# Joining the small matrix products of both tiles of a chunk into common runs, in a DeltaNet and GELU kernel

## The chip, the cores and the metric

The kernel runs on one core of a Trainium2 chip. The metric is the time of one execution on the device, in microseconds (us). The engines are named as the profile names them: PE (TensorE, matrix products; PEld is its loading of weights), DVE (VectorE), ACT (ScalarE), POOL (GpSimd) and SP (SyncE, which issues most transfers). Each engine works through its own list of instructions in order and waits on semaphores for the others. Matrix products land in PSUM, which DVE and ACT empty.

## The reference

There are two stages. The first is a delta-rule attention over 4 batches, 8 heads, 768 steps and a head width of 48; the second is a feed-forward block over the resulting 3072 x 384 matrix, with an exact GELU between its two products.

```
for t in range(S):
    y[:, :, t] = einsum('bhd,bhde->bhe', q[:, :, t], state)
    v_old = einsum('bhde,bhd->bhe', state, kt)      # kt: the normed key
    state = state + bt * einsum('bhd,bhe->bhde', kt, vt - v_old)
x = y.transpose(0, 2, 1, 3).reshape(B * S, H * D)
h = x @ w_in                                        # 384 x 2048
out = (0.5 * h * (1 + erf(h / sqrt(2)))) @ w_out    # 2048 x 384
```

All is fp32 (the two weights arrive as 8-byte floats and are decoded to fp32 on the chip). Each fp32 matrix product of the program stands in the trace as two MATMUL records.

## The kernel before

The steps are cut into 12 chunks of 64. A tile is one chunk of two batches: 8 heads, 48 wide, with the 64 steps of one batch on the lower and of the other on the upper half of the 128 partitions. A chunk has two tiles (`NA = 2`), called a0 and a1 below. Two chunks make a group. Inside a chunk the recurrence is written as small products, one for each head and half:

- `transposed` (L276) turns K and Q of a tile (psT, 128 x 128 transposes); `products` (L286) makes K K^T and K Q^T at once (psG, the Gram products). ACT copies the K K^T half to `G` (L301), `pack` (L309) copies three pieces of `G` into `diag`, DVE masks the other half into `P` (L307).
- `eliminate_steps` (L339) inverts the 32 x 32 diagonal blocks of a whole group on DVE: one transpose and one multiply over 1024 columns, 30 pairs of multiply and add (L359, L361), three transposes back (L370, L374). `join` (L391) then makes the 64 x 64 inverses from the 32 x 32 ones by two levels of 32 x 32 products (psJ, L404 and L407). Each call does one chunk of the group: DVE scales the first level (L415), ACT copies the second (L419).
- `against_state` (L450) is K S (psK) and then two DVE operations that give W (L459, L460); `query` (L477) is Q S (psQ), copied by ACT to y (L485); `solve` (L463) is U (psU), copied by ACT in four pieces (L475); `next_state` (L503) is K^T U (psS), added to the state by DVE (L512); `read` (L487) is P^T U (psY), added to y by DVE in four pieces (L501); `turn` (L514) transposes the result for the feed-forward block (psX).

The feed-forward block of a chunk is `fc1` (L532: 16 times three products of 128 x 128 with 256 columns, psH, then GELU on ACT, L538) and `fc2` (L540: 32 products with 384 columns, psO). The products of the attention use only part of the PE: 64 x 64 or 32 x 32 of its 128 x 128. In the text a tiled run is a stretch of such products between two stretches of full-size ones (psH, psO, and the transposes psT and psX).

PSUM holds two buffers of two banks for all tiled products (`dn`), two banks for psT and psX (`sq`) and two for psH and psO (`mlp`). The program first writes chunk 0 in an order by hand (L581 to L648), then a plan (L659 to L686) gives each step a due time in chunks, and sorts all steps by it: `state_steps`, `gram_steps` and `join_steps` return (weight, step) pairs that `at` spreads between two times. DVE keeps that order; for the other engines a scheduler orders the instructions as their inputs come free. The weights are decoded on DVE and ACT (`decode`, `signed`, L186 to L208) during chunks 0 and 1.

Of the kernel before, what the change touches and what calls it, by code (L numbers as in the profile page):

```python
# [8 lines left out]
F32 = mybir.dt.float32  # L9
# [7 lines left out]
def kernel(  # L17
# [28 lines left out]
    nc = tc.nc  # L46
# [239 lines left out]
    def products(u, part=(0, 1)):  # L286
# [9 lines left out]
        if 0 in part:  # L296
            if u.t == 0:
                Gs[g] = wk.tile([128, 2 * NA, H, C], F32, tag="G", name="G", bufs=1)
            if u.t == 0 and g > 0:
                Ds[g] = wk.tile([128, NU, HB], F32, tag="diag", name="diag", bufs=1)  # L300
            nc.scalar.copy(heads(Gs[g][:, u.t]), psG[:, :, :, 0:C])  # L301
# [7 lines left out]
    def pack(u, copy=nc.scalar.copy):  # L309
        g = u.c // 2  # L310
        span = slice(u.t * H, (u.t + 1) * H)
        copy(Ds[g][:, span], Gs[g][:, u.t, :, 0:HB])
        for p in range(2):
            lower = slice(p * C + HB, (p + 1) * C)
            copy(Ds[g][lower, span], Gs[g][lower, u.t, :, HB:C])
# [3 lines left out]

    def gram(u):  # L320
        products(u)
        pack(u)
# [68 lines left out]
    def join(g, ts, level, copy=nc.scalar.copy):  # L391

        xm, zf, raw = XMs[g], Zf[g % 2], Gs[g].rearrange("q t h n -> q (t h) n")
        gm = gms[g].rearrange("q t h -> q (t h)")
        psJ = dn("psJ")
        us = range(ts[0] * H, (ts[-1] + 1) * H)
        span = slice(us[0], us[-1] + 1)
        for i, u in enumerate(us):
            for p in range(2):
                top = slice(p * C, p * C + HB)  # L400
                low_ = slice(p * C + HB, (p + 1) * C)
                col = slice(i * HB, (i + 1) * HB)
                if level == 0:
                    nc.tensor.matmul(psJ[low_, 0, col], lhsT=raw[top, u, HB:C],  # L404
                                     rhs=xm[top, u, :], start=True, stop=True)
                else:
                    nc.tensor.matmul(psJ[top, 0, col], lhsT=xm[low_, u, :],  # L407
                                     rhs=zf[low_, u, HB:C], start=True, stop=True)
        for p in range(2):
            top = slice(p * C, p * C + HB)  # L410
            low_ = slice(p * C + HB, (p + 1) * C)
            rows = top if level else low_
            src = psJ[rows, 0, 0:len(us) * HB].rearrange("q (u n) -> q u n", n=HB)
            if level == 0:
                nc.vector.tensor_tensor(  # L415
                    xm[low_, span, :], src,
                    gm[low_, span].unsqueeze(2).to_broadcast([HB, len(us), HB]), op=ALU.mult)
            else:
                copy(zf[top, span, HB:C], src)  # L419
# [22 lines left out]
    def state_product(u, x, psum):  # L442

        for j in range(NP):
            for r, p in QUADS:
                rows = slice(r * C, r * C + D)
                nc.tensor.matmul(psum(p, j, r), lhsT=u.KQt[rows, j, p, x, :],  # L447
                                 rhs=St[rows, u.a, p, j, :], start=True, stop=True)

    def against_state(u):  # L450
        u.W = wk.tile([128, H, D], F32, tag="W", name="W")
        gm = gms[u.c // 2][:, u.t]
        if u.c == 0:
            nc.gpsimd.tensor_tensor(u.W, u.V, ng[:, u.a].unsqueeze(2).to_broadcast([128, H, D]),
                                    op=ALU.mult)
            return
        psK = dn("psK")[:, :, 0:NP * D].rearrange("q r (j d) -> q r j d", d=D)
        state_product(u, 0, lambda p, j, r: psK[HALF[p], r, j, :])
        nc.vector.tensor_tensor(heads(u.W), psK, heads(u.V), op=ALU.subtract)  # L459
        nc.vector.tensor_tensor(u.W, u.W, gm.unsqueeze(2).to_broadcast([128, H, D]),  # L460
                                op=ALU.mult)

    def solve(u, copies=(nc.scalar.copy,)):  # L463
        zf = Zf[(u.c // 2) % 2]
        psU = dn("psU")[:, :, 0:DM].rearrange("q p (h d) -> q p h d", d=D)
        for k in range(NP // 2):
            for r in range(2):
                for p, s in SIDES:
                    h = 4 * k + 2 * s + r
                    nc.tensor.matmul(psU[HALF[p ^ s], p, h, :],  # L470
                                     lhsT=zf[HALF[p], u.t * H + h, :], rhs=u.W[HALF[p], h, :],
                                     start=True, stop=True)
        u.U = wk.tile([128, H, D], F32, tag="U", name="U")
        for i, (p, s) in enumerate(SIDES):
            copies[i % len(copies)](pairs(u.U[HALF[p]], s), pairs(psU[HALF[p ^ s], p], s))  # L475

    def query(u):  # L477
        u.y = None
        if u.c == 0:
            return  # L480
        psQ = dn("psQ")[:, :, 0:NP * D].rearrange("q r (k s d) -> q k s r d", s=2, d=D)
        state_product(u, 1, lambda p, j, r: psQ[HALF[p ^ (j % 2)], j // 2, j % 2, r, :])
        u.y = wk.tile([128, H, D], F32, tag="y", name="y")
        for r in range(2):
            nc.scalar.copy(heads(u.y)[:, r], psQ[:, :, :, r, :].rearrange("q k s d -> q (k s) d"))  # L485

    def read(u, copies=(nc.scalar.copy,)):  # L487
        psY = dn("psY")[:, :, 0:DM].rearrange("q p (h d) -> q p h d", d=D)
        for k in range(NP // 2):
            for r in range(2):  # L490
                for p, s in SIDES:
                    h = 4 * k + 2 * s + r
                    nc.tensor.matmul(psY[HALF[p ^ s], p, h, :], lhsT=u.P[HALF[p], h, :],  # L493
                                     rhs=u.U[HALF[p], h, :], start=True, stop=True)
        u.x = wk.tile([128, H, D], F32, tag="x", name="x")
        for i, (p, s) in enumerate(SIDES):
            dst, src = pairs(u.x[HALF[p]], s), pairs(psY[HALF[p ^ s], p], s)
            if u.y is None:
                copies[i % len(copies)](dst, src)
            else:  # L500
                nc.vector.tensor_tensor(dst, src, pairs(u.y[HALF[p ^ s]], s), op=ALU.add)  # L501

    def next_state(u):  # L503
        if u.c == NC - 1:
            return
        psS = dn("psS")[:, :, 0:NP * D].rearrange("q p (j d) -> q p j d", d=D)
        for j in range(NP):
            for r, p in QUADS:
                nc.tensor.matmul(psS[HALF[r], p, j, :],  # L509
# [207 lines left out]
```

## Time and profile before

| | |
|---|---|
| time, three runs | 756.45 us median (755.42 to 761.29) |
| the profiled execution's own time | 755.02 us |
| its span on the core | 753.3 us |
| chunk 0, by hand | to about 60 us |
| decoding of the weights on DVE | to about 141 us |
| first join of a whole group on PE | at 170.70 us |
| last product on PE ends | at about 749 us |

The profile is of one execution, and the sums of the prediction are made against it. Its views: the page's busy shares, the chain of work that ended last, a table of busy time by stretch of time, groups of instructions (line, engine, operation, output<-input, shape, count, then busy us and mean ns of one, then idle time ahead of them and what ended it), a timeline (start, duration, engine, line, operation, output<-input, shape, count of records) and a list of who waited for whom. A MATMUL's duration in the timeline includes its way through the array, so from one group of matmuls to the next the difference of the starts is what counts.

### The profile page before, as it was taken

The numbers are of one execution on the slowest core, as the hardware profiler recorded it, in microseconds if no ns is written. First come the engines' busy times: TensorE is split into PE (matmuls) and PEld (weight loads), VectorE is DVE, ScalarE is ACT, GpSimd is POOL, SyncE is SP. The second block draws the span as 40 slices with busy tenths as digits, with TensorE's granted clock in tenths as the row PEclk, the third lists the DMA queues.
The fourth block names the chain that finished last, engine by engine and source line by source line (L and its number), as shares of the span: only waits on it lengthen the run. The fifth ranks groups of instructions, "written<-read, shape, count | busy, mean of one in ns | idle before, by whom it ended". The sixth has DMA issues, their size and how long they took to land.

```text
span 753.3 us, 19282 instructions
## 1 busy us (share of the span) xinstructions
PE 704.0 (93%) x8532; PEld 508.5 (68%) x8532; DVE 376.4 (50%) x855; ACT 249.4 (33%) x602; POOL 84.7 (11%) x91
## 2 busy tenths in 40 slices
PE   6549786899999999999999999999999999999997
PEld 5347553576687687687587687687687687586774
DVE  6988999996329722329822329822329821210100
ACT  3335633422553134352134352133352132122120
POOL 5051001203110002110012010012020010000000
PEclk9999999998999999999999999999999999999999
DMA  9807544400311101211101211001001000000000
GB/s 150 199 25 206 131 125 129 103 1 19 60 33 23 32 13 32 44 32 23 34 13 32 44 32 23 12 12 23 12 12 23 12 12 2 11 12 1 22 1 21
DMA packets 84515, 32.90 MB, mean 44 GB/s; under 512 B 77328, under 2 KB 80400, under 8 KB 84432
## 3 DMA queue, kind: packets, MB, share of 16 engines
q1 hardware_dynamic: 78384, 26.36, 16.0%
q10 hardware_dynamic: 5952, 5.12, 3.0%
q8 instruction: 67, 1.10, 0.6%
q0 software_dynamic: 96, 0.20, 0.1%
q14 instruction: 16, 0.13, 0.1%
HBM read 26.94 MB, written 4.72 MB: 42 GB/s over the span
## 4 chain that ended last, share of the span: by engine, by line
PE 77%; DVE 19%; issue 2%; DMA 1%; POOL 1%; ACT 0%; ACTq 0%; POOLq 0%; DVEq 0%
PE psO L544 30%; PE psH L535 30%; DVE tmp L359 3%; DVE Nu L361 3%; PE psT L283 2%; PE psG L293 2%; DVE w_e L204 2%; PE psU L470 2%; PE psJ L404 2%; PE psS L509 2%; PE psQ L447 2%; PE psK L447 2%; PE psJ L407 2%; PE psY L493 1%; DVE w_e L194 1%
## 5 line engine op out<-in xcount | busy, mean ns | idle before, releaser
L544 PE MATMUL psO<-w_out_sb,g 128*128 128x384 f32 x768 | 272.9, 500 | 10.2 <-DVE w_out_sb L205 10.2
L535 PE MATMUL psH<-xT,w_in_sb 128*128 128x256 f32 x1152 | 274.9, 388 | 3.4 <-DVE w_in_sb L205 3.0
L535 PEld LDWEIGHTS psH<-xT,w_in_sb 128*128 128x128 f32 x1152 | 213.1, 191 | 37.4 <-DVE w_in_sb L205 3.5
L544 PEld LDWEIGHTS psO<-w_out_sb,g 128*128 128x128 f32 x768 | 140.4, 192 | 97.2 <-DVE w_out_sb L205 15.6
L538 ACT ACTIVATE g<-psH 128x256 f32<-128x256 f32 x192 | 73.5, 383 | 177.4 <-PE psH L535 177.1
L361 DVE TENSOR_TENSOR Nu<-Nu,tmp 128x30 f32<-128x30 f32 (+9 forms) x180 | 61.9, 344 | 6.2
L359 DVE TENSOR_TENSOR tmp<-Nu 128x30 f32<-128x30 f32 (+9 forms) x180 | 61.8, 343 | 5.6
L253 POOL TENSOR_TENSOR n<-n,half 128x16 f32<-128x16 f32 x10 | 29.5, 2947 | 222.6 <-DVE n L242 222.6
L501 DVE TENSOR_TENSOR x<-psY,y 64x192 f32<-64x192 f32 x88 | 31.0, 353 | 42.3 <-PE psY L493 41.4
L307 DVE TENSOR_TENSOR P<-psG,mask 128x512 f32<-128x512 f32 x20 | 13.7, 690 | 72.8 <-ACT G L301 72.7
L512 DVE TENSOR_TENSOR St<-St,psS 128x384 f32<-128x384 f32 x22 | 12.2, 553 | 75.4 <-PE psS L509 75.0
L459 DVE TENSOR_TENSOR W<-psK,V 128x384 f32<-128x384 f32 x22 | 12.2, 555 | 73.6 <-PE psK L447 56.8
L475 ACT COPY U<-psU 64x192 f32<-64x192 f32 x92 | 28.8, 313 | 46.8 <-PE psU L470 46.0
L548 ACT COPY o_sb<-psO 128x384 f32<-128x384 f32 x24 | 11.5, 479 | 89.3 <-PE psO L544 89.3
L293 PE MATMUL psG<-KQt 48*64 48x128 f32 (+1 forms) x896 | 30.4, 286 | 3.9 <-ACT KQt L284 2.7
L522 ACT COPY xT<-psX 128x384 f32<-128x384 f32 x24 | 11.4, 477 | 68.0 <-PE psX L521 67.9
L293 PEld LDWEIGHTS psG<-KQt 48*64 48x64 f32 x896 | 24.9, 157 | 10.6 <-issue 4.8
L284 ACT COPY KQt<-psT 128x512 f32<-128x512 f32 x48 | 26.5, 589 | 9.1 <-PE psT L283 8.6
L383 POOL MEMSET Zf<- 32x512 f32 x23 | 12.2, 529 | 147.5 <-DVE Zf L374 145.5
L404 PE MATMUL psJ<-XM,G 32*32 32x32 f32 x768 | 15.5, 198 | 13.6 <-DVE XM L370 13.6
L415 DVE TENSOR_TENSOR XM<-psJ,gm 32x512 f32<-32x512 f32 (+1 forms) x26 | 16.9, 649 | 20.4 <-PE psJ L404 20.1
L196 ACT ACTIVATE w_e<-w_e,lim 128x384 uint32<-128x384 uint32 (+2 forms) x31 | 19.4, 625 | 23.0 <-DVE w_e L194 22.8
(100 smaller groups left out, 584.9 us busy)
## 6 DMA issues: line engine op xcount, KB each, us to landing
Qp<-in_q_dram SPq DMA_DIRECT2D x48, 96.0 KB, 3.4
V<-in_v_dram SPq DMA_DIRECT2D x48, 96.0 KB, 2.9
w_out_sb<-in_moe_w_in_dram SPq DMA_DIRECT2D x9, 512.0 KB, 5.3
out_dram<-o_sb ACTq DMA_DIRECT2D x48, 96.0 KB, 2.2
Zf<-in_moe_w_out_dram SPq DMA_DIRECT2D x8, 384.0 KB, 3.5
w_raw<-in_moe_w_out_dram SPq DMA_DIRECT2D x8, 384.0 KB, 3.1
Kp<-in_k_dram SPq DMA_DIRECT2D x28, 96.0 KB, 3.1
w_out_sb<-in_moe_w_in_dram SPq DMA_DIRECT2D x6, 256.0 KB, 4.4
```

Source lines behind the costliest of these rows:

```text
L253: nc.gpsimd.tensor_tensor(flat, flat, half, op=ALU.pow)
L284: nc.scalar.copy(u.KQt[:, :, :, x, :], psT.rearrange("q j (p n) -> q j p n", p=2))
L293: nc.tensor.matmul(psG[HALF[p], r, j, cols], lhsT=u.KQt[rows, j, p, 0, :], rhs=u.KQt[rows, j, p].rearrange("q x n -> q (x n)")[:, cols], s ...
L359: nc.vector.tensor_tensor(tmp, nu[:, j + 1:, j:j + 1].to_broadcast([128, n, j]), nu[:, j:j + 1, 0:j].to_broadcast([128, n, j]), op=ALU.mult)
L361: nc.vector.tensor_tensor(nu[:, j + 1:, 0:j], nu[:, j + 1:, 0:j], tmp, op=ALU.add)
L404: nc.tensor.matmul(psJ[low_, 0, col], lhsT=raw[top, u, HB:C], rhs=xm[top, u, :], start=True, stop=True)
L447: nc.tensor.matmul(psum(p, j, r), lhsT=u.KQt[rows, j, p, x, :], rhs=St[rows, u.a, p, j, :], start=True, stop=True)
L475: copies[i % len(copies)](pairs(u.U[HALF[p]], s), pairs(psU[HALF[p ^ s], p], s))
L501: nc.vector.tensor_tensor(dst, src, pairs(u.y[HALF[p ^ s]], s), op=ALU.add)
L535: nc.tensor.matmul(psH, lhsT=w_in_sb[:, m, f * 128:(f + 1) * 128], rhs=xTs[c][:, m, :], start=(m == 0), stop=(m == NM - 1))
L538: nc.scalar.activation(gs[f], psH, ACT.Gelu)
L544: nc.tensor.matmul(u.psO, lhsT=gs[f][:, u.a * 128:(u.a + 1) * 128], rhs=w_out_sb[:, f, :], start=(f == 0), stop=(f == NF - 1))
```

## The change

The small products of both tiles are made one after the other, without full-size products in between, and what belongs together lands in one PSUM buffer: K S and Q S of a tile in one (`psK`), U of both tiles in one (`psU`), P^T U and K^T U of a tile in one (`psY`, `psS`). The Gram products of both tiles follow each other, and ACT now takes only the needed quarter blocks from them. A `join` level does a whole group at once.

```
 def products(u, part=(0, 1)):
...
-            nc.scalar.copy(heads(Gs[g][:, u.t]), psG[:, :, :, 0:C])
+            nc.scalar.copy(heads(Gs[g][:, span]), psG[:, :, :, HB:C])
+            if g > 0:
...
+                nc.scalar.copy(heads(Ds[g][:, span]), psG[:, :, :, 0:HB])
+                for p in range(2):
+                    lower = slice(p * C + HB, (p + 1) * C)
+                    nc.scalar.copy(Ds[g][lower, span], Gs[g][lower, span])
...
-    def pack(u, copy=nc.scalar.copy):
...
-    def gram(u):
-        products(u)
-        pack(u)
+    def grams(us):
+        for u in us:
+            products(u)
...
     def gram_steps(c):
         us = [tiles[c, a] for a in range(NA)]
-        return [(1.0, fn, u) for fn in (transposed, gram) for u in us]
+        return [(1.0, transposed, u) for u in us] + [(2.0, grams, us)]
...
     def join_steps(g):
-        return [(1.0, join, g, (2 * cc, 2 * cc + 1), level)
-                for level in range(2) for cc in range(2)]
+        return [(1.0, join, g, range(2 * NA), level) for level in range(2)]
...
+    def against_state(us):
+        for u in us:
...
+            u.psK = dn("psK")[:, :, 0:2 * NP * D].rearrange("q r (x j d) -> q x r j d", x=2, d=D)
+            for x in range(2):
+                for j in range(NP):
+                    for r, p in QUADS:
+                        rows = slice(r * C, r * C + D)
+                        to = HALF[p ^ (j % 2)] if x else HALF[p]
+                        nc.tensor.matmul(u.psK[to, x, r, j, :], lhsT=u.KQt[rows, j, p, x, :],
+                                         rhs=St[rows, u.a, p, j, :], start=True, stop=True)
+        for u in us:
...
+            nc.vector.tensor_tensor(heads(u.W), u.psK[:, 0], heads(u.V), op=ALU.subtract)
+            nc.vector.tensor_tensor(u.W, u.W, gm.unsqueeze(2).to_broadcast([128, H, D]),
                                     op=ALU.mult)
...
+                nc.scalar.copy(heads(u.y)[:, r], u.psK[:, 1, r])
...
+    def use(us):
+        for u in us:
+            psY = dn("psY")
+            u.psY = quarters(psY[:, :, 0:NP * D])
+            u.psS = psY[:, :, NP * D:2 * NP * D].rearrange("q p (j d) -> q p j d", d=D)
...
+            if u.c > 0:
+                update(u)
...
+    def outputs(us):
+        use(us)
+        for u in us:
+            next_state(u)
+            read(u)
...
     def state_steps(c):
         us = [tiles[c, a] for a in range(NA)]
-        steps = [(1.0, fn, u) for fn in (against_state, query, solve, next_state, read) for u in us]
+        steps = [(3.0, against_state, us), (2.0, solve, us), (3.0, outputs, us)]
         return steps + [(0.5, turn, u) for u in us]
...
     decode(0)
-    solve(first[0], on[0])
     decode(1)
-    solve(first[1], on[1])
+    solve(first[:NA], on)
     signed(0)
-    read(first[0], on[0])
+    use(first[:NA])
+    for u in first[:NA]:
+        read(u, on[u.a])
     decode(2)
     signed(1)
-    read(first[1], on[1])
     signed(2)
```

`solve` makes the products of both tiles and then copies them; `update` holds the K^T U products that `next_state` had, and `next_state` keeps the addition. No product is added or removed. The order of instructions changes in three kinds of places.

On PE, the joins and the products with the state in chunk 4, before (psK and psQ are K S and Q S of a tile, psH is fc1; x9 counts products of the program):

```order
L404 MATMUL psJ<-XM,G 32x32 x32
L535 MATMUL psH<-xT,w_in_sb 128x256 x3
L407 MATMUL psJ<-Zf_126,XM 32x32 x32
L535 MATMUL psH<-xT,w_in_sb 128x256 x6
L407 MATMUL psJ<-Zf_126,XM 32x32 x32
L535 MATMUL psH<-xT,w_in_sb 128x256 x9
L447 MATMUL psK<-St,KQt 64x48 x16
L535 MATMUL psH<-xT,w_in_sb 128x256 x6
L447 MATMUL psK<-St,KQt 64x48 x16
L535 MATMUL psH<-xT,w_in_sb 128x256 x6
L447 MATMUL psQ<-St,KQt 64x48 x16
L535 MATMUL psH<-xT,w_in_sb 128x256 x6
```

The same place on PE in the changed program (psK now holds K S and Q S of a tile, x64 is both tiles):

```order
L548 MATMUL psH<-xT,w_in_sb 128x256 x6
L399 MATMUL psJ<-XM,G 32x32 x64
L548 MATMUL psH<-xT,w_in_sb 128x256 x9
L399 MATMUL psJ<-Zf_126,XM 32x32 x64
L548 MATMUL psH<-xT,w_in_sb 128x256 x21
L452 MATMUL psK<-St,KQt 64x48 x64
L548 MATMUL psH<-xT,w_in_sb 128x256 x12
```

Eight tiled runs (four joins, two K S, two Q S) have become three, with the fc1 products gathered between them. The U products go from two runs to one, and K^T U with P^T U from four to one. From the first join of a whole group to the end, PE enters a tiled run from a full-size product 122 times before and 48 times now. Also, the 16 transposes of chunk 4 (psT, four for each of K and Q of both tiles), which stood behind that join, now stand before it.

On ACT, the copies of y in chunk 4 before, with what each waits for (g is the GELU of an fc1 result, PE_49 and DVE_49 are the engines' semaphores):

```order
L538 ACTIVATE g_3285<-psH 128x256 [waits PE_49]
L485 COPY y<-psQ 128x4x48 [waits PE_49]
L485 COPY y<-psQ 128x4x48
L538 ACTIVATE g_3311<-psH 128x256 [waits PE_49]
L538 ACTIVATE g_3317<-psH 128x256 [waits PE_49]
L485 COPY y<-psQ 128x4x48 [waits PE_49]
L485 COPY y<-psQ 128x4x48
```

The same place on ACT now:

```order
L551 ACTIVATE g_3202<-psH 128x256 [waits PE_49]
L551 ACTIVATE g_3208<-psH 128x256 [waits PE_49]
L463 COPY y<-psK 128x4x48 [waits DVE_49]
L463 COPY y<-psK 128x4x48
L463 COPY y<-psK 128x4x48 [waits DVE_49]
L463 COPY y<-psK 128x4x48
L551 ACTIVATE g_3301<-psH 128x256 [waits PE_49]
```

The copies of y wait for DVE, which reads K S of the same buffer first, and the GELUs stand behind them.

On DVE, in the part by hand, before (x is the result of chunk 0's tile a1, w_e and w_in_sb belong to the decoding, St is the state):

```order
L475 COPY U<-psU 64x2x96 x4
L204 SCALAR_TENSOR_TENSOR w_e<-w_out_sb,w_e 128x256
L205 SCALAR_TENSOR_TENSOR w_in_sb<-w_in_sb,w_e 128x256
L194 TENSOR_SCALAR w_e<-w_out_sb 128x256
L197 TENSOR_SCALAR w_in_sb<-w_out_sb 128x256
L199 SCALAR_TENSOR_TENSOR w_in_sb<-w_out_sb,w_in_sb 128x256
L204 SCALAR_TENSOR_TENSOR w_e<-w_out_sb,w_e 128x256
L205 SCALAR_TENSOR_TENSOR w_in_sb<-w_in_sb,w_e 128x256
L499 COPY x<-psY 64x2x96 x4
L204 SCALAR_TENSOR_TENSOR w_e<-w_out_sb,w_e 128x256
L205 SCALAR_TENSOR_TENSOR w_in_sb<-w_in_sb,w_e 128x256
L512 TENSOR_TENSOR St<-St,psS 128x384 x2
```

And now:

```order
L484 COPY U<-psU 64x2x96 x4
L204 SCALAR_TENSOR_TENSOR w_e<-w_out_sb,w_e 128x256
L205 SCALAR_TENSOR_TENSOR w_in_sb<-w_in_sb,w_e 128x256
L517 COPY x<-psY 64x2x96 x4
L194 TENSOR_SCALAR w_e<-w_out_sb 128x256
L197 TENSOR_SCALAR w_in_sb<-w_out_sb 128x256
L199 SCALAR_TENSOR_TENSOR w_in_sb<-w_out_sb,w_in_sb 128x256
L204 SCALAR_TENSOR_TENSOR w_e<-w_out_sb,w_e 128x256
L205 SCALAR_TENSOR_TENSOR w_in_sb<-w_in_sb,w_e 128x256
L204 SCALAR_TENSOR_TENSOR w_e<-w_out_sb,w_e 128x256
L205 SCALAR_TENSOR_TENSOR w_in_sb<-w_in_sb,w_e 128x256
L510 TENSOR_TENSOR St<-St,psY 128x384 x2
```

The copy of x has moved ahead of five decoding operations. In the planned part of DVE's list, W of both tiles now stand together, as do P of both tiles, and the addition to the state stands right before each tile's four additions to y.

More of the change, by code (lines that the diff above doesn't have):

```diff
@@ L495, in read, with update, next_state @@
+    def update(u):
+        if u.c < NC - 1:
+            for j in range(NP):
+                for r, p in QUADS:
+                    nc.tensor.matmul(u.psS[HALF[r], p, j, :], lhsT=u.Kp[HALF[p], 2 * j + r, :],
+                                     rhs=u.U[HALF[p], 2 * j + r, :], start=True, stop=True)
+    def next_state(u):
+        if u.c < NC - 1:
+            nc.vector.tensor_tensor(St[:, u.a], St[:, u.a], u.psS, op=ALU.add)
+    def read(u, copy=nc.scalar.copy):
         u.x = wk.tile([128, H, D], F32, tag="x", name="x")
-        for i, (p, s) in enumerate(SIDES):
-            dst, src = pairs(u.x[HALF[p]], s), pairs(psY[HALF[p ^ s], p], s)
+        for p, s in SIDES:
+            dst, src = pairs(u.x[HALF[p]], s), u.psY[HALF[p ^ s], p]
@@ L645 @@
     for u in first[:NA]:
+        update(u)
         next_state(u)
@@ L661 @@
     plan += [at(0.98, 0.985, [(1.0, load, 3)]),
-             at(1.02, 1.1, [(1.0, join, 0, (2, 3), level) for level in range(2)]),
+             at(1.02, 1.1, [(1.0, join, 0, range(NA, 2 * NA), level) for level in range(2)]),
 ]
```

151 lines of the change are left out of this document (60 added, 91 removed).

## The prediction

> **What bounds the kernel now.** I read the page first (busy shares, slices, chain), then the table by stretch, then PE's timeline in a stretch of each kind.
>
> ```profile
> span 753.3 us, 19282 instructions
> ...
> PE 704.0 (93%) x8532; PEld 508.5 (68%) x8532; DVE 376.4 (50%) x855; ACT 249.4 (33%) x602; POOL 84.7 (11%) x91
> ...
> PE 77%; DVE 19%; issue 2%; DMA 1%; POOL 1%; ACT 0%; ACTq 0%; POOLq 0%; DVEq 0%
> ```
> ```profile
> 60.00:103.00 43.00, 38.69 (x568) 29.25 (x561) 41.27 (x88) 25.39 (x58) 3.12 (x1) 0.96 0.60 144
> 146.00:171.00 25.00, 23.14 (x121) 19.28 (x122) 22.91 (x64) 6.33 (x17) 0.00 (x0) 1.00 0.13 31
> 264.00:321.00 57.00, 56.79 (x815) 41.36 (x814) 13.93 (x29) 21.01 (x51) 8.83 (x7) 1.00 0.15 29
> ```
> ```profile
> 170.70 2.79 PE L404 MATMUL psJ<-XM,G 32*32 32x32 f32 x128 [1.86 <-DVE XM L370]
> ```
>
> The columns of the table are the stretch, its length, and the busy time of PE, PEld, DVE, ACT and POOL, then the granted clock. There are two stages. Up to 170.70 us DVE decodes and eliminates almost without a pause (41.27 of 43.00 us), and PE ends that stage by waiting 1.86 us for DVE's XM. From there to the end PE is busy without gaps (56.79 of 57.00 us, granted clock 1.00), while DVE and ACT have room. So in the first stage only DVE's list counts, in the second only what PE has to do.
>
> **What a tiled run costs.** PE's timeline in the second stage:
>
> ```profile
> 393.66 0.68 PE L447 MATMUL psK<-St,KQt 48*64 48x48 f32 x32
> 394.27 2.86 PE L535 MATMUL psH<-xT,w_in_sb 128*128 128x256 f32 x12
> 397.06 0.68 PE L447 MATMUL psK<-St,KQt 48*64 48x48 f32 x32
> ...
> 440.21 2.76 PE L535 MATMUL psH<-xT,w_in_sb 128*128 128x256 f32 x12
> 442.90 1.10 PE L293 MATMUL psG<-KQt 48*64 48x128 f32 x32
> ```
> ```profile
> 200.06 0.68 PE L509 MATMUL psS<-U,Kp 64*64 64x48 f32 x32
> 200.56 1.07 PE L293 MATMUL psG<-KQt 48*64 48x128 f32 x32
> 201.45 0.68 PE L493 MATMUL psY<-U,P 64*64 64x48 f32 x32
> 202.06 0.91 PE L544 MATMUL psO<-w_out_sb,g 128*128 128x384 f32 x2
> ```
> ```profile
> 707.52 20.88 PE L535 MATMUL psH<-xT,w_in_sb 128*128 128x256 f32 x96
> 728.24 20.80 PE L544 MATMUL psO<-w_out_sb,g 128*128 128x384 f32 x64
> ```
>
> Undisturbed, 96 fc1 records take 728.24 - 707.52 = 20.72 us, so twelve take 2.59. Twelve that come from transposes and end at a tiled run take 442.90 - 440.21 = 2.69: entering the run costs 0.10. Twelve between two tiled runs take 397.06 - 394.27 = 2.79: coming back costs another 0.10. Inside, a run of 32 records that is followed by fc1 takes 394.27 - 393.66 = 0.61, but one that is followed by other tiled products only 200.56 - 200.06 = 0.50: the last 0.11 is paid once for each run, however long. Each run thus has a fixed price of 0.10 + 0.10 + 0.11 = 0.31 us beside its products. For the 32 x 32 joins I take the same price, without a row of their own.
>
> The row that could contradict the 0.11 is the longer run of one kind that the trace has:
>
> ```profile
> 88.99 1.15 PE L470 MATMUL psU<-W,Zf 64*64 64x48 f32 x64
> ```
>
> Against 0.68 for 32 records, the second 32 cost 0.47, so the fixed part is 0.14 by this row. I take 0.11, since it comes from starts and not from modelled ends, and keep 0 and 0.14 as ends; 0 because no row has 128 tiled records of one kind at full clock.
>
> The Trainium skill speaks against the change here: TensorE: Matmul & The Clock Gate, section "Wait — 56ns, not 53.3ns?", says that matmuls never start less than about 25 ns apart, however few columns they have. By that, tiled products would be bought one by one and a longer run would save nothing inside; only the 0.20 of entering and coming back would go, and the sum would be 740. The rows differ: 0.50 us for 32 records is 15.6 ns each.
>
> **The change part by part.** (1) In the second stage the runs entered from full-size products go from 122 to 48. Entering and the fixed part: (122 - 48) x 0.21 = 15.5. Coming back: before, 107 runs are followed by psH or psO (0.10 each), 5 by a transpose psT and 10 by psX; now all 48 by psH or psO. psT and psX pay less:
>
> ```profile
> 185.15 0.66 PE L283 MATMUL psT<-ident,Kp 128*128 128x128 f32 x4
> 185.64 0.60 PE L283 MATMUL psT<-ident,Qp 128*128 128x128 f32 x4
> ...
> 437.17 0.60 PE L283 MATMUL psT<-ident,Kp 128*128 128x128 f32 x4
> 437.60 0.60 PE L283 MATMUL psT<-ident,Qp 128*128 128x128 f32 x4
> ```
>
> Right behind a tiled run four transposes take 185.64 - 185.15 = 0.49, else 437.60 - 437.17 = 0.43: 0.06. For psX I take 0 (its ends 0 and 0.06 are 0.6 us apart in all). So 10.7 + 0.3 - 4.8 = 6.2. Together 21.7 us less; with 0 for the fixed part 13.6, with 0.14 24.0.
>
> (2) The 16 transposes of chunk 4 move from behind 170.70 to ahead of it, four groups of 0.43: 1.7 us less in the second stage. In the first they lie beside fc2 products that wait for decoding, and PE waits for DVE at its end anyway, so they cost nothing there; without that cover it would be the 1.7 again.
>
> (3) In the part by hand the copy of x (a1) comes earlier on DVE, and with it psX, K^T U and the addition to the state:
>
> ```profile
> 57.34 0.90 PE L521 MATMUL psX<-ident,x 128*128 128x128 f32 x3 [1.64 <-DVE x L499]
> 58.17 1.96 PE L509 MATMUL psS<-U,Kp 64*64 64x48 f32 x64
> ...
> 55.83 1.45 DVE L499 COPY x<-psY 64x192 f32<-64x192 f32 x4
> ...
> 59.34 0.56 DVE L512 TENSOR_TENSOR St<-St,psS 128x384 f32<-128x384 f32 x1 [1.14 <-PE psS L509]
> 60.20 0.56 DVE L512 TENSOR_TENSOR St<-St,psS 128x384 f32<-128x384 f32 x1 [0.30 <-PE psS L509]
> ```
>
> PE sits 1.64 us before psX waiting for that copy, and DVE 1.14 + 0.30 = 1.44 us for K^T U. The copy now follows its product at once, which costs DVE a wait of some 0.4 us for psY; K^T U comes about 1.2 us earlier. I take 1.0 us less on DVE (ends 0 and 1.4), and since DVE's list is full up to 170.70, all of it arrives there.
>
> (4) The rest of DVE's list to 170.70 keeps its operations in another order, and DVE waits wherever PE is late. W of both tiles is now one block at about the place of the second W, where K S and Q S of both tiles have long been asked for; the two P stand three operations behind the first one's old place; the state's additions stand later than K^T U was before. I count 0, and up to 3 us more as an end.
>
> (5) New waits in the second stage, from the groups of the page:
>
> ```profile
> L501 DVE TENSOR_TENSOR x<-psY,y 64x192 f32<-64x192 f32 x88 | 31.0, 353 | 42.3 <-PE psY L493 41.4
> ...
> L512 DVE TENSOR_TENSOR St<-St,psS 128x384 f32<-128x384 f32 x22 | 12.2, 553 | 75.4 <-PE psS L509 75.0
> ...
> L475 ACT COPY U<-psU 64x192 f32<-64x192 f32 x92 | 28.8, 313 | 46.8 <-PE psU L470 46.0
> ...
> L415 DVE TENSOR_TENSOR XM<-psJ,gm 32x512 f32<-32x512 f32 (+1 forms) x26 | 16.9, 649 | 20.4 <-PE psJ L404 20.1
> ```
> ```profile
> L538 ACT ACTIVATE g<-psH 128x256 f32<-128x256 f32 x192 | 73.5, 383 | 177.4 <-PE psH L535 177.1
> ...
> L419 ACT COPY Zf<-psJ 32x512 f32<-32x512 f32 (+1 forms) x26 | 14.1, 542 | 19.2 <-PE psJ L407 19.0
> ```
>
> U of both tiles is eight copies, 2.5 us, behind which PE has 8 or 12 fc2 products (0.65 each by the row above) before it asks for U: covered. The first join level is four scalings on DVE, 2.6 us, under 9 fc1 products, 3.9: covered by 1.3. A tile's addition to the state and its four to y take 0.55 + 4 x 0.35 = 2.0 on DVE, two tiles 4.0; where the Gram products follow after four fc2 products (2.6 + 0.2), they need both psY buffers back. The second buffer is free about 1.0 + 4.0 = 5.0 us after the run began, and PE comes there at 2.0 + 2.8 + 0.9 = 5.7: the thinnest cover; each us more on DVE would cost up to 5 us over five groups. The second join level is four copies on ACT, 4 x 0.54 = 2.2, and a GELU behind them, 0.38: 2.6 us and two hand-overs, about what two fc1 groups keep PE busy (2.6 + 0.2); I take 0.2 us for each of five groups. I count 1.0 us for (5), with ends 0 and 5.
>
> Sum against the profiled execution: 755.0 - 21.7 - 1.7 - 1.0 + 0 + 1.0 = 731.6. It lies 1.4 us below the median of the runs shown, about the spread of their lower half, so I forecast 732.
>
> **The rivals.** (a) The fixed part inside a run doesn't go, or small waits take its place: 13.6 in place of 21.7 gives 740, with the ends of (4) and (5) as well 747. For it: no long run of one kind at full clock is in the trace. Against it: the 0.50 and 0.47.
>
> (b) PE's clock. In the trace it halves after a short wait:
>
> ```profile
> 170.30:177.50 7.20, 6.80 (x134) 4.54 (x134) 7.08 (x9) 0.00 (x0) 2.07 (x4) 0.61 0.02 3
> 177.50:208.00 30.50, 29.98 (x583) 20.70 (x583) 10.72 (x28) 14.60 (x35) 7.47 (x4) 0.98 0.25 48
> ```
>
> After 1.86 us of waiting, 0.61 of the clock was granted for 7 us, which costs some 3 us. If 2 us of tiled products count as waiting, each such spell of 3.4 us would lose 1.7; one in each of ten chunks gives 732 + 17 = 749, two 766. Against it: the tiled stretch of 2.0 us from 200.06 lies in a stretch with 0.98.
>
> The Trainium skill describes this gate (TensorE: Matmul & The Clock Gate, Part 1): it watches PE in a free-running window of about 3.4 us and halves the clock after an idle one. No run here shows yet whether tiled products count as busy in it.
>
> (c) Slower: ACT's copies of y wait for DVE's subtraction and the GELUs stand behind them, so PE runs out of psH buffers after two fc1 groups, 2.6 us. DVE would have to reach W more than 2.6 us after K S is made; the gain is used up at 2.6 + 23.4/10 = 4.9 us late in each of ten chunks, and at 5.5 the time would be 732 + 10 x 2.9 = 761.
>
> ```profile
> DVE W L459 <- PE psK L447: 56.8, 11, 9.9
> ```
>
> Against it: DVE waited for K S in 11 of 22 cases, 56.8 us in all, and K S now comes later after the Gram products (21 fc1 products against 9).
>
> **How the numbers follow.** The forecast 0.70, (a) 0.18, (b) 0.05, (c) 0.04; 0.03 stays for what I don't see, put to no change. The likeliest case alone spans 728 to 737. The low end, 726, takes 0.14 for the fixed part, 1.4 for (3) and no new waits (755.0 - 24.0 - 1.7 - 1.4 = 728), and a spell of half clock less (2); the high end, 747, is the far end of (a). Faster by over 1% (below 748.9) holds with the forecast and (a), 0.88; within 1% gets 0.06 (one spell of (b) in a chunk, and the unseen), slower 0.06 ((c) and two spells). One per cent is about what a measurement of this kernel can tell from no change.
>
> **What would show it.** The chain has the first join of two successive groups, 113.5 us apart:
>
> ```profile
> 264.52 1.13 PE psJ L404 x64
> ...
> 378.06 1.13 PE psJ L404 x64
> ```
>
> Two chunks have 26 runs now and 10 after, so 16 x 0.31 = 5.0 us less. Right: in the second stage a run of 64 records of U takes about 1.1 us from start to start, the 128 of psK 2.1, fc1 and fc2 keep their 2.59 for twelve and eight, two chunks take about 108.5 us, and the first whole join starts near 169.7. Wrong: PE gaps behind psG, psH or psJ released by DVE or ACT; a granted clock below 1 beyond 180 us; 16 ns a record that turn into 19.

## The result and the profile after

| | before | after |
|---|---|---|
| time, four runs each | 755.93 us median (753.33 to 761.29) | 729.15 us median (728.83 to 729.88) |
| the profiled execution's own time, its span | 755.02, 753.3 | 729.33, 727.6 |
| first join of a whole group starts | 170.70 | 171.61 |
| from there to the end of the span | 582.6 | 556.0 |

The ratio is 0.9638, with a 95% interval of 0.9585 to 0.9691: the change makes the kernel faster. In the second stage 26.6 us went; in the first 0.9 us came on top. Of the kernel after, these are the busy shares and the chain of the page, and the three stretches that were shown of the kernel before (stretch, length, busy time of PE, PEld, DVE, ACT and POOL, then the granted clock):

```profile
span 727.6 us, 19244 instructions
...
PE 681.1 (94%) x8532; PEld 511.0 (70%) x8532; DVE 372.2 (51%) x855; ACT 241.4 (33%) x602; POOL 84.7 (12%) x91
...
PE 76%; DVE 17%; DMA 2%; ACT 2%; issue 2%; POOL 1%; ACTq 0%; SPq 0%; POOLq 0%; DVEq 0%
```
```profile
60.00:103.00 43.00, 38.02 (x588) 29.37 (x586) 40.91 (x87) 24.81 (x59) 3.12 (x1) 0.92 0.59 148
146.00:171.00 25.00, 22.07 (x98) 18.36 (x97) 22.75 (x63) 5.78 (x16) 0.12 (x1) 1.00 0.16 35
264.00:321.00 57.00, 56.94 (x717) 43.47 (x716) 11.92 (x30) 23.04 (x57) 7.46 (x4) 1.00 0.18 35
```

The same 8532 records keep PE busy 22.9 us less (704.0 to 681.1). DVE is still busy almost throughout the first stage, and PE without gaps in the second (56.94 of 57.00 us), at full clock. This is PE's timeline there (start, duration, line, operation, shape, count of records, two for each product):

```profile
474.02 2.75 PE L548 MATMUL psH<-xT,w_in_sb 128*128 128x256 f32 x12
476.71 2.21 PE L399 MATMUL psJ<-XM,G 32*32 32x32 f32 x128
478.85 4.15 PE L548 MATMUL psH<-xT,w_in_sb 128*128 128x256 f32 x18
482.93 2.21 PE L399 MATMUL psJ<-Zf,XM 32*32 32x32 f32 x128
485.08 9.66 PE L548 MATMUL psH<-xT,w_in_sb 128*128 128x256 f32 x42
494.66 2.08 PE L452 MATMUL psK<-St,KQt 48*64 48x48 f32 x128
496.67 5.45 PE L548 MATMUL psH<-xT,w_in_sb 128*128 128x256 f32 x24
501.96 0.60 PE L283 MATMUL psT<-ident,Kl 128*128 128x128 f32 x4
...
505.51 1.15 PE L478 MATMUL psU<-W,Zf 64*64 64x48 f32 x64
506.59 2.85 PE L557 MATMUL psO<-w_out_sb,g 128*128 128x384 f32 x8
...
540.83 9.47 PE L548 MATMUL psH<-xT,w_in_sb 128*128 128x256 f32 x42
550.23 2.08 PE L452 MATMUL psK<-St,KQt 48*64 48x48 f32 x128
...
584.99 2.21 PE L399 MATMUL psJ<-XM,G 32*32 32x32 f32 x128
```

From start to start, 128 records of K S and Q S take 496.67 - 494.66 = 2.01 and 64 of U 506.59 - 505.51 = 1.08, so 64 more records cost 0.93, 14.6 ns each, and 0.14 is left as the fixed part of either run. Eighteen fc1 records between two runs take 4.08, which is 18 x 0.2158 + 0.20. Two chunks take 584.99 - 476.71 = 108.28 where they took 113.54. Two things are not as they should be: 42 fc1 records between two runs should take 42 x 0.2158 + 0.20 = 9.26, but behind the second join level they take 494.66 - 485.08 = 9.58, and behind the Gram products 550.23 - 540.83 = 9.40.

In the first stage DVE's waits changed. Its list of waits (line, who it waited for, us in total, times, longest) between 30 and 165 us, before and after:

```profile
DVE U L475 <- PE psU L470: 1.5, 1, 1.5
DVE St L512 <- PE psS L509: 1.4, 2, 1.1
```
```profile
DVE U L484 <- ACT U L484: 2.9, 1, 2.9
DVE w_e L194 <- DMA w_out_sb<-in_moe_w_in_dram: 0.6, 1, 0.6
DVE x L517 <- PE psY L496: 0.4, 1, 0.4
```

The 1.4 us for K^T U went, as forecast. In its place DVE waits 1.4 us longer for U, and what releases it is no longer PE's products but ACT's copies. It also waits 0.4 for P^T U, and 0.6 for a weight near 76 us. The program's list for DVE says why it waits for ACT: its first copy of U waited for one semaphore before, and waits for two now.

```
before:  COPY U<-psU 64x2x96 [waits PE_49]
after:   COPY U<-psU 64x2x96 [waits PE_49,Activation_49]
```

### The profile page after: what moved, and what is told of

Read it like the earlier page. It is cut to its first block, busy times and chain, and to the rows that moved or that the text cites. A ratio compares the mean times of both kernels' runs of the same rounds, so it can differ in the third digit from the quotient of the medians.

```text
span 727.6 us, 19244 instructions
## 1 busy us (share of the span) xinstructions
PE 681.1 (94%) x8532; PEld 511.0 (70%) x8532; DVE 372.2 (51%) x855; ACT 241.4 (33%) x602; POOL 84.7 (12%) x91
## 4 chain that ended last, share of the span: by engine, by line
PE 76%; DVE 17%; DMA 2%; ACT 2%; issue 2%; POOL 1%; ACTq 0%; SPq 0%; POOLq 0%; DVEq 0%
PE psO L557 32%; PE psH L548 28%; PE psJ L399 3%; DVE tmp L357 3%; DVE Nu L359 3%; PE psK L452 3%; PE psG L293 2%; PE psT L283 2%; PE psU L478 2%; PE psY L496 2%; DVE w_e L204 2%; PE psY L505 1%; ACT Zf L414 1%; DVE w_out_sb L205 1%; DVE w_out_sb L199 1%
## 5 line engine op out<-in xcount | busy, mean ns | idle before, releaser
L557 PE MATMUL psO<-w_out_sb,g 128*128 128x384 f32 x768 | 265.4, 494 | 5.2 <-DVE w_out_sb L205 5.1
L548 PE MATMUL psH<-xT,w_in_sb 128*128 128x256 f32 x1152 | 266.4, 387 | 3.7 <-DVE w_in_sb L205 2.2
L548 PEld LDWEIGHTS psH<-xT,w_in_sb 128*128 128x128 f32 x1152 | 216.6, 192 | 40.1 <-ACT g L551 4.5
L557 PEld LDWEIGHTS psO<-w_out_sb,g 128*128 128x128 f32 x768 | 142.0, 192 | 95.5 <-DVE w_out_sb L205 10.0
L510 DVE TENSOR_TENSOR St<-St,psY 128x384 f32<-128x384 f32 x22 | 12.1, 552 | 71.2 <-PE psY L505 70.9
L293 PE MATMUL psG<-KQt 48*64 48x128 f32 (+1 forms) x896 | 28.7, 285 | 4.2 <-ACT KQt L284 2.7
L273 POOL TENSOR_TENSOR V<-V,n 128x384 f32<-128x384 f32 x20 | 16.8, 845 | 108.7 <-DMA V<-in_v_dram 88.3
```

The source lines that it names most:

```text
L293: nc.tensor.matmul(psG[HALF[p], r, j, cols], lhsT=u.KQt[rows, j, p, 0, :], rhs=u.KQt[rows, j, p].rearrange("q x n -> q (x n)")[:, cols], s ...
L548: nc.tensor.matmul(psH, lhsT=w_in_sb[:, m, f * 128:(f + 1) * 128], rhs=xTs[c][:, m, :], start=(m == 0), stop=(m == NM - 1))
L557: nc.tensor.matmul(u.psO, lhsT=gs[f][:, u.a * 128:(u.a + 1) * 128], rhs=w_out_sb[:, f, :], start=(f == 0), stop=(f == NF - 1))
```

## The experiments

There are two theories for the second stage. Either each tiled run has a fixed price, so that the gain follows the number of runs; or the gain comes from the packing in PSUM, which leaves fewer buffers to hand over and fewer copies. The first three kernels keep the packing and take runs apart again. All times below are medians of four to six runs, with the ratio to the kernel before on the same chip. Differences to the changed kernel are against its 729.15 us where nothing else is said; its repeat on the chip of the first four experiments (below) gave 728.12, so that those differences are 1 us larger on one chip.

**Joins by chunk again.**

```
-        return [(1.0, join, g, range(2 * NA), level) for level in range(2)]
+        return [(0.5, join, g, range(cc * NA, (cc + 1) * NA), level)
+                for level in range(2) for cc in range(2)]
```

> The joins of a group go back to one run per chunk of the group, everything else as after the change: 56 tiled runs entered from full-size products in the second stage in place of 48. If a run has a fixed price (113.54 - 108.28 = 5.26 us less for two chunks with 16 runs less: 0.33 us each), the stretch from the first whole join to the end grows from 556.0 to 558.6 us and the time is 2.6 us above the changed kernel, about 731.8. If the gain came from the packing (fewer buffers to hand over, fewer copies) and not from the number of runs, it stays within 0.5 us of 729.2.

730.01 us (728.48 to 731.03), ratio 0.9666 (0.9642 to 0.9689). From the first whole join to the end of the span it is 728.5 - 170.90 = 557.6, so +1.6 and not +2.6. That alone settles nothing: the same stretch takes 556.0 in the first trace of the changed kernel and 725.7 - 170.97 = 554.7 in its repeat. The timeline, further on, tells more:

```profile
475.68 1.20 PE L399 MATMUL psJ<-XM,G 32*32 32x32 f32 x64
476.81 2.86 PE L549 MATMUL psH<-xT,w_in_sb 128*128 128x256 f32 x12
479.59 1.20 PE L399 MATMUL psJ<-XM,G 32*32 32x32 f32 x64
...
487.26 8.04 PE L549 MATMUL psH<-xT,w_in_sb 128*128 128x256 f32 x36
495.23 2.08 PE L453 MATMUL psK<-St,KQt 48*64 48x48 f32 x128
```

The runs have their price: 64 records take 476.81 - 475.68 = 1.13, so two runs take 2.26 in place of 2.14, and the twelve fc1 records between them 2.78 in place of 2.59. But the fc1 records behind the last one take 495.23 - 487.26 = 7.97, exactly 36 x 0.2158 + 0.20. The 0.32 us that the joint version takes longer there (9.58 - 9.26) are gone. So in two chunks 2 x 0.32 us of price stand against 0.32 of a wait that goes: 108.59 us against 108.28.

**The state's steps tile by tile again.**

```
-        steps = [(3.0, against_state, us), (2.0, solve, us), (3.0, outputs, us)]
+        steps = [(w_, fn, [u]) for w_, fn in ((1.5, against_state), (1.0, solve), (1.5, outputs))
+                 for u in us]
```

> The steps of the state (K S with Q S, U, P^T U with K^T U) are emitted tile by tile again, each result where the change packed it: 72 runs in the second stage in place of 48. With a fixed price of 0.33 us a run the time is 7.9 us above the changed kernel, about 737, and two chunks take 108.3 + 1.6 = some 110 us or more (24 runs over 10 chunks: 4.8 runs for two chunks, 1.6 us). If packing made the gain, it stays within 2 us of 729.2.

741.98 us (741.82 to 742.22), ratio 0.9828 (0.9812 to 0.9843): 12.8 us above the changed kernel, more than the 7.9 of the price. Part of the rest is a new wait:

```profile
PE psY L496 <- DVE P L313: 1.9, 3, 0.6
```

Where P^T U of a tile follows the Gram products at once, it needs the PSUM buffer that DVE still reads for P.

**Everything apart.** Both edits, and the Gram products as two steps in place of one.

> State steps, Gram products and joins all emitted one tile (joins: one chunk) at a time, with the packing of the change: 91 runs in the second stage in place of 48. Fixed price per run: 43 x 0.33 = 14.2 us above the changed kernel, about 743.4; the three doses (8, 24, 43 runs) lie on one line. If packing made the gain: within 4 us of 729.2, and no line.

743.07 us (742.51 to 743.85), ratio 0.9842 (0.9826 to 0.9859): 13.9 us above, 14.2 were expected. With 19 runs more than the kernel ahead it is only 1.1 us slower, since that kernel has several waits and this one next to none. So the kernels are compared in the steady part, two chunks from join to join, less the waits that the timelines show there (0.32 behind the joint second level, 0.14 behind joint Gram products, 0.76 behind P, about 0.3 for x in the kernel before):

| kernel | runs in two chunks | two chunks, us | waits | without waits | per run over 10 |
|---|---|---|---|---|---|
| after | 10 | 108.28 | 0.46 | 107.82 | |
| joins by chunk | 12 | 108.59 | 0.14 | 108.45 | 0.32 |
| state by tile | 15 | 110.79 | 1.22 | 109.57 | 0.35 |
| all apart | 20 | 111.12 | 0 | 111.12 | 0.33 |
| before | 26 | 113.55 | 0.3 | 113.25 | 0.34 |

They lie on one line of 0.32 to 0.35 us a run. The packing is the same in the first four, so it isn't what is gained.

**Joint without packing.** What packing does do is asked from the other side: this is the kernel before, with only the order of the steps joined.

```
-        steps = [(1.0, fn, u) for fn in (against_state, query, solve, next_state, read) for u in us]
+        def both(*fns):
+            for fn in fns:
+                for u in us:
+                    fn(u)
+        steps = [(4.0, both, against_state, query), (2.0, both, solve), (4.0, both, next_state, read)]
```

> The kernel before with one edit: the state steps of a chunk's two tiles are emitted together, each result still in a buffer of its own (Gram products and joins as before). With only two PSUM buffers for tiled results the joint runs break up at Q S: 74 runs in the second stage in place of 122. If only the number of runs counts, 48 x 0.33 = 15.8 us below the kernel before, about 740. If PE now waits for the buffers (a K S of the second tile behind DVE's subtraction of the first, and so on: 1 to 2 us for each of ten chunks), 10 to 20 us of that are lost again and the time is 750 or more, with PE idle ahead of psK, psQ, psS or psY in the list of waits.

750.74 us (749.04 to 753.29), ratio 0.9945 (0.9926 to 0.9963). Two chunks have 16 runs and take 113.21 us; by the line they would take 107.82 + 6 x 0.34 = 109.86. Some 3.0 of the 3.3 us between are waits by its timeline; PE's list of waits behind 178 us names them (9.9 us over the whole stage):

```profile
PE psY L493 <- DVE St L512: 5.5, 9, 1.2
PE psS L509 <- DVE P L307: 2.2, 3, 0.7
PE psQ L447 <- DVE W L459: 2.2, 10, 0.3
```

So both theories have a part, in different roles: the price of the runs is what is gained, and the packing is what lets the runs be joined without waiting for the two buffers.

**Does a record have a floor of its own?** Each product of U is issued twice, and the same result is written again.

```
+                        for again in range(2):
+                            nc.tensor.matmul(u.psU[HALF[p ^ s], p, k, r, :],
```

> The changed kernel with each of the products of U issued twice (the same result written again): 640 records more in the second stage, in the same 48 runs. If a run has a fixed price and its records 14.6 ns each, a run of 128 records of U takes 1.08 + 64 x 0.0146 = 2.01 us from start to start and the time is 9.3 us above the changed kernel, about 738.5. By the 25 ns floor of the Trainium skill (TensorE: Matmul & The Clock Gate, the section on 56 ns) the run would take 1.08 + 1.6 = 2.7 us and the time would be 745.

740.81 us (739.53 to 740.93), ratio 0.9806 (0.9788 to 0.9825), 12.7 us above the changed kernel on the same chip (728.12, below).

```profile
511.55 2.18 PE L479 MATMUL psU<-W,Zf 64*64 64x48 f32 x128
513.66 2.85 PE L558 MATMUL psO<-w_out_sb,g 128*128 128x384 f32 x8
```

The run takes 513.66 - 511.55 = 2.11, so 64 records more cost 1.03, 16 ns each (14.6 were expected): 10.3 us over ten chunks. Another 1.7 lie in the first stage, where the first whole join comes at 172.66 in place of 170.97 (the repeat, below). The 25 ns from start to start that the Trainium skill states (TensorE: Matmul & The Clock Gate, "Wait — 56ns, not 53.3ns?") do not hold for these records.

**U of chunk 0 in two buffers.** This one is about the first stage.

```
-    solve(first[:NA], on)
+    for u in first[:NA]:
+        solve([u], on[u.a:])
```

> The changed kernel with one edit: in the part by hand, U of the two tiles of chunk 0 go to two PSUM buffers again. If DVE's copies of U of tile 1 waited there for ACT's copies of tile 0 because both read one buffer (DVE idle 2.90 us before them, against 1.55 before the change), they start near 51.8 in place of 53.13 us; the fetch behind the first decoding goes out earlier, DVE's 0.59 us wait for a weight near 76 us goes or shrinks, and the first whole join comes 1.3 to 2.0 us earlier than 171.61: near 170. The time is then up to 2 us below 729.2, unless PE's clock behind that wait takes some back. If the loss came from the other order of the operations and not from the shared buffer, the join stays at 171.6 and the time at 729.

727.55 us (726.26 to 728.0), ratio 0.9629 (0.9615 to 0.9643). DVE's copies of U (timeline, in brackets the idle time ahead and who ended it), in the changed kernel and here:

```profile
53.13 1.46 DVE L484 COPY U<-psU 64x192 f32<-64x192 f32 x4 [2.90 <-ACT U L484]
```
```profile
51.85 1.46 DVE L484 COPY U<-psU 64x192 f32<-64x192 f32 x4 [1.54 <-PE psU L478]
...
169.92 2.85 PE L399 MATMUL psJ<-XM,G 32*32 32x32 f32 x128 [2.13 <-DVE XM L368]
```

DVE waits for PE again, its copies start 1.28 us earlier, and the first whole join comes at 169.92, where the kernels that share this part by hand with the changed one have it at 170.73 to 171.17 (leaving out those in which DVE waited over 0.5 us for a weight, and the doubled U). The shared buffer was the cause of the wait. The time as a whole hardly shows it: 727.55 us here, 728.12 in the repeat of the changed kernel on another chip.

**The changed kernel once more**, to see whether the wait for a weight belongs to it.

> The changed kernel once more, on the chip of the next two, so that they are compared on one chip: within 1 us of 729.2. In most of the traces so far that share its part by hand DVE waited for no weight near 76 us and the first whole join came at 170.7 to 171.2; if the 0.59 us wait of the first trace was chance, the join now comes near 171.0, otherwise at 171.6 again.

728.12 us (727.41 to 728.81), ratio 0.9642 (0.9624 to 0.966).

```profile
53.05 1.46 DVE L484 COPY U<-psU 64x192 f32<-64x192 f32 x4 [2.91 <-ACT U L484]
...
170.97 2.64 PE L399 MATMUL psJ<-XM,G 32*32 32x32 f32 x128 [2.50 <-DVE XM L368]
```

The wait for U is there again, the wait for the weight isn't. The latter was 0.6 us in the first trace, 2.5 in that of the kernel with the later join (below), and 0.3 or less in every other: it varies from one execution to the next. So without that wait the change leaves the first whole join about where it was (170.70 before, 170.97 now), and two buffers for U move it to 169.92. The second stage is 1.3 us shorter than in the first trace (554.7 against 556.0), and the timelines put all of it at its beginning, where PE's clock is cut behind its wait for the join: two traces of one kernel differ by that much there.

**The wait behind the second join level.** The four copies of that level are made by DVE in place of ACT, so that no GELU stands behind them.

```
-        return [(1.0, join, g, range(2 * NA), level) for level in range(2)]
+        return [(1.0, join, g, range(2 * NA), level, nc.vector.tensor_copy) for level in range(2)]
```

> The changed kernel with the four copies behind the second level of each whole join on DVE in place of ACT. From starts in the changed kernel's trace, 42 fc1 products behind that level take 9.58 us where 42 with a tiled run on both sides should take 42 x 0.2158 + 0.20 = 9.26: 0.32 us, once a group. If that is GELU waiting behind ACT's copies, they take 9.27 now and the time is 4 or 5 times 0.32 = 1.3 to 1.6 us below 729.2. If it is a fixed price of the long run itself, the 9.58 stay and so does the time.

727.40 us (726.31 to 728.34), ratio 0.9629 (0.9615 to 0.9644).

```profile
482.57 9.33 PE L548 MATMUL psH<-xT,w_in_sb 128*128 128x256 f32 x42
491.83 2.08 PE L452 MATMUL psK<-St,KQt 48*64 48x48 f32 x128
```

491.83 - 482.57 = 9.26: the 0.32 are gone, to the hundredth, and two chunks take 107.96. It was the GELUs behind ACT's copies.

**The first whole join later.** PE waits some 3 us for DVE ahead of that join, while fc2 products are at hand.

```
-             at(2.5, 2.62, join_steps(1)), at(2.62, 2.97, state_steps(2)),
+             at(2.6, 2.7, join_steps(1)), at(2.7, 2.97, state_steps(2)),
```

> The changed kernel with the due time of the first whole join moved from 2.5 to 2.6: eight more fc2 products (2.6 us at full clock) stand ahead of it, where PE waited 3.54 us for DVE. The products fill the wait, so 2.6 us are gained if DVE stays where it is (join at 171.6, PE idle about 0.9 before it). If the half clock behind the wait comes from the wait, it goes too: the first join takes 2.2 in place of 3.56 and the eight fc2 behind it 2.8 in place of 4.20, another 2.7 us: 724 in all. If the clock is cut anyway there: 726.6. If U and Gram back to back then make PE wait for PSUM buffers: 1 to 2 us of it are lost.

727.96 us (727.7 to 728.72), ratio 0.9636 (0.962 to 0.9652). That is hardly a gain.

```profile
173.10 2.41 PE L399 MATMUL psJ<-XM,G 32*32 32x32 f32 x128 [1.01 <-DVE XM L368]
175.44 4.26 PE L557 MATMUL psO<-w_out_sb,g 128*128 128x384 f32 x8
...
190.31 1.07 PE L293 MATMUL psG<-KQt 48*64 48x128 f32 x32
193.19 1.10 PE L293 MATMUL psG<-KQt 48*64 48x128 f32 x32 [1.81 <-ACT U L484]
```

The edit also put U and the Gram products of chunk 4 into one run. That saves one price, 0.34, and costs 1.81: the second tile's Gram products need the buffer from which ACT copies U. In this trace DVE also had its 2.5 us for the weight, so the join came late, at 173.10; and the clock was cut behind PE's wait all the same (4.26 us for eight fc2 records that take 2.85 at full clock).

**The three edits together, and with the Gram products spaced.** The second kernel has one edit more, the Gram products of chunk 4 due a little later:

```
-             at(2.6, 2.61, [(1.0, prep, 4)]), at(2.65, 2.9, gram_steps(4))]
+             at(2.6, 2.61, [(1.0, prep, 4)]), at(2.7, 3.0, gram_steps(4))]
```

> The three edits together: U of chunk 0 in two buffers, the copies behind the second join level on DVE, the first whole join behind eight more fc2 products. The gains should add where they lie in different places: 729.2 - 1.5 - 1.4 - 4 = about 722; the first and third overlap, since an earlier join leaves PE less of a wait to fill, so 723 is as likely. Above 726 the three would be in each other's way.

> As the kernel with the three edits, with the Gram products of chunk 4 due a little later, so that they follow the run of P^T U in place of the run of U (where their second buffer waited 1.81 us for ACT's copies of U). If that wait was the price of the missing products between, it goes: 1.6 to 1.8 us below 725.6, about 724, and no PE wait ahead of psG after the first join. If a wait of the same size comes up behind P^T U (its two buffers are held by DVE for about 4 us, of which 2.8 lie under fc2), the time stays at 725.6.

With the three edits the time is 725.63 us (725.39 to 727.05), ratio 0.961 (0.9596 to 0.9625), and the same 1.81 us wait behind U. With the Gram products spaced it is 722.28 us (721.81 to 722.35), ratio 0.9563 (0.9546 to 0.9579), and PE's list of waits from 168 us to the end holds only

```profile
PE psJ L399 <- DVE XM L368: 1.0, 1, 1.0
PE psJ L399 <- DVE XM L410: 0.7, 2, 0.5
```

More came back (3.4 us) than the wait of 1.81. The stretch from 178 to 205 us, with three edits and then spaced, shows the rest:

```profile
178.00:205.00 27.00, 25.19 (x460) 17.07 (x453) 12.41 (x30) 9.38 (x26) 5.27 (x4) 0.94 0.20 39
```
```profile
178.00:205.00 27.00, 27.00 (x498) 19.64 (x491) 12.33 (x30) 12.01 (x32) 5.45 (x4) 1.00 0.27 53
```

Behind the wait the granted clock was cut to 0.94 over the stretch, 27 x 0.06 = 1.6 us; 1.81 + 1.6 = 3.4; the one run more takes 0.34 of it back, so some 0.3 of the gain stays open. The 1.6 is no fixed price of that wait: the kernel with the later join had the same wait and no cut clock behind it (last section). The two kernels ran on two chips, on which the kernel before took 755.55 and 755.37 us. The spaced version is 5.8 us faster than the changed kernel on the same chip and beats both kernels.

## Why the prediction was right, and where it was not

The forecast was 732 us, 726 to 747, faster; 729.15 were measured. Its steps follow one by one, against the profiled executions (755.02 to 729.33, so 25.7 us less, where the sum had 23.4):

1. *Runs entered in the second stage, 122 to 48.* The mechanism holds, by the line of the table over kernels with the same packing. The size was off: the fixed part inside a run is 0.14, the end that the row of 64 records of U gave, and not the 0.11 taken. With it the term is 24.0 in place of 21.7. The 0.11 was the difference of two runs of 32 records, 0.61 and 0.50, and the second of them still holds some 0.03 beside 32 x 14.6 ns.
2. *Transposes of chunk 4 ahead of the join.* They were counted with 1.7, and the trace of after has them there; no experiment separates them.
3. *The part by hand, -1.0 us.* This step failed: the first whole join came 0.9 later in the first trace and 0.3 later in the repeat. The gain it named came (the 1.4 us wait for K^T U went), but a wait of the same size took its place: DVE's copies of U of tile 1 wait for ACT's copies of tile 0, since both now read one buffer. The prediction looked at where the operations stand in DVE's list, not at the semaphores that a shared buffer adds. The Trainium skill has the rule (PSUM — Partial Sum Buffer, "PSUM bank collisions raise a hardware error"): two engines may not touch the same PSUM bank in the same 32 partitions at once, two reads included, and so a scheduler makes one wait. The 2.90 us behind ACT fit that; what would happen without the wait wasn't tried. With two buffers the join comes at 169.92; 169.7 was forecast.
4. *The rest of DVE's list, 0.* This was right but for the 0.6 us wait for a weight, which the second trace of the same kernel hasn't.
5. *New waits in the second stage, +1.0.* The place was right (GELU behind the second join level), the size 0.32 in place of 0.2 for each of four groups; the first group, followed by fc2, doesn't have it. Another 0.14 behind joint Gram products, four times, wasn't foreseen, and no experiment asked for its cause: 1.8 us in all. The thin cover of psY's buffers held.

Put together, the second stage has 24.0 + 1.7 - 1.8, and three gains that the sum did not have, taken from the starts in the two timelines: 0.2 that PE loses less at the cut clock at its beginning (3.1 before, 2.8 after), some 0.6 of a wait for ACT's copies of U there, and 1.1 that PE no longer waits for x (three times 0.36). That makes 25.8 of the 26.6; the other 0.8 is not accounted for. The first stage gives back 0.9. So 2.3 (the fixed part) and 1.9 (the gains left out) went one way, 1.9 (the first stage) and 0.8 (the new waits) the other. That the forecast came as near as it did is in part luck, since these errors cancel in part.

Of the rivals, (a), that the fixed part isn't saved, is refuted by the 2.01 us for 128 records. (b), that the joined runs bring a halved clock, did not happen: the granted clock is 1.00 in every stretch of the second stage from 205 us on, with 2.0 us of tiled products in a row (the two lines below). Whether such products count as busy for the clock is not shown by that, since no run in these stretches is longer than 2.2 us.

```profile
205.00:445.00 240.00, 239.89 (x3064) 183.77 (x3063) 110.25 (x249) 85.32 (x220) 28.21 (x23) 1.00 0.16 31
445.00:625.00 180.00, 179.89 (x2378) 134.75 (x2377) 85.70 (x193) 55.24 (x145) 17.06 (x17) 1.00 0.08 16
```

(c), that ACT's copies of y wait for DVE's W, does happen, by ACT's list of waits:

```profile
ACT y L463 <- DVE W L458: 20.3, 21, 2.1
```

At 2.1 us at most it stays under the 2.6 that two fc1 groups cover, and costs PE nothing: the 24 fc1 records behind K S and Q S take 501.96 - 496.67 = 5.29, which is 24 x 0.2158 + 0.10, the price of coming back.

## What to carry to other kernels

Small products that use a part of the array cost a fixed price each time PE turns to them and back, here 0.34 us (0.10 + 0.14 + 0.10), so count the turns, and join the runs as far as the PSUM buffers allow without waiting. Putting two runs together is worth only that price: look at what the evictions behind it hold up (0.32 us of GELU ate half of the joined join levels, 1.81 us of buffer wait five times the price). And where results of two tiles move into one buffer, look in the program at the semaphores of every reader: engines that emptied two buffers side by side may now take turns.

## What the runs showed of the hardware

PE's clock behind a short wait was cut in one run and not in another. Ahead of the first whole join PE waited 1.01 us in the kernel with the later join, and the eight fc2 records after the join took 4.26 (2.85 at full clock); it waited 1.03 us in the last kernel, and they took 2.85:

```profile
170.23 2.21 PE L399 MATMUL psJ<-XM,G 32*32 32x32 f32 x128 [1.03 <-DVE XM L368]
172.38 2.85 PE L557 MATMUL psO<-w_out_sb,g 128*128 128x384 f32 x8
```

The wait of 1.81 us between the Gram products of chunk 4 shows the same. The kernel with the later join and the kernel with three edits have it in the same order of products, and these are the eight fc2 records behind it, first in the one and then in the other:

```profile
194.22 2.85 PE L557 MATMUL psO<-w_out_sb,g 128*128 128x384 f32 x8
```
```profile
190.70 4.54 PE L557 MATMUL psO<-w_out_sb,g 128*128 128x384 f32 x8
```

So the length of the wait alone doesn't decide it. The Trainium skill says that the gate looks through a free-running window of about 3.4 us (TensorE: Matmul & The Clock Gate, Part 1), so that the phase would count; no run here shows the window. By the same section of the Trainium skill the clock is cut after an idle window. Here a wait of about 1 us was followed by a cut once, but 175.44 - 173.10 = 2.3 us of tiled products stood between the two, and no run tells whether they count as idle.

And 32 x 32, 48 x 64 and 64 x 64 products of 32 to 48 columns cost about the same, 14.6 to 16 ns a record beside the fixed part (2.01 us for 128 of K S and Q S, 2.14 for 128 of a join).
